# Attention and two expert layers in one kernel: the first block's q loaded in four DMAs instead of one, and k and v of batch 1 loaded on 128 partitions instead of 96

## The chip, the core and the metric

The kernel runs on one core of a Trainium2 chip, as one launch. The metric is the device time of that launch in microseconds (us). Engines are named as the profile names them: PE (matmuls), PEld (weight loads of PE), DVE, ACT, POOL, and SP, which here only issues DMAs.

## The reference

What is computed, cut to what matters (batch 4, 8 heads, 576 positions, head size 64; 2304 tokens, width 512, inner widths 2048 and 1024, all in float32):

```python
kv = einsum('bhsd,bhse->bhde', k, v)
out = einsum('bhsd,bhde->bhse', q, kv)
x = out / sqrt(mean(out * out, -1) + 1e-06) * g_norm    # then heads side by side: 2304 x 512
h = x @ w_in
x = (h * tanh(log1p(exp(h)))) @ w_out                   # 512 -> 2048 -> 512
h = x @ w2_in                                           # 512 -> 1024
solu = h * softmax(h)
return layernorm(solu) * g_ln @ w2_out                  # 1024 -> 512
```

## The kernel before

**Tiling.** The 2304 tokens are cut into six blocks of 384 (`BLK`), three tiles of 128 each. A batch has 576 positions, so block 0 lies in batch 0, and block 1 takes the end of batch 0 and the start of batch 1. Every large matmul is done as three float16 passes on a high and a low half of each operand (`PASS`).

**The start, block 0.** k and v of a batch come in four pairs of heads, (b, 0) to (b, 3), each two DMAs of 288 KB (`load_pair`, L238 to L249). For a batch in `WIDE` (L168, batch 0 alone) a head's 576 rows lie on 64 partitions, nine rows on each, so that two heads fill 128 partitions and a partition gets one run of 2304 bytes; `kv_pair` (L273 to L287, matmuls L286) then does 18 float32 matmuls of 64 rows by 64 columns. For the other batches the rows lie on 96 partitions, six on each, for both heads: two runs of 1536 bytes and 12 matmuls of 96 rows. Block 0's q is one DMA of 768 KB for all eight heads (`load_q`, L253). For each pair of heads c, PE transposes q (qTp, L317), multiplies it with kv (xoT, L331), sums the squares (L342), spreads the inverse root (rT<-ident,rho, L362, after POOL's power at L354, which follows DVE's small addition at L348), and DVE multiplies (xf, L373) and takes low halves (xT, L382).

**The start, block 1 on.** q of block 1 is two DMAs of 384 KB, which wait until all of block 0's q has been transposed. ACT makes its high halves (qhl, L398), DVE the low ones (L403), and SP issues a transposing DMA for each of the three tiles (L411). kv of batch 1 becomes two float16 halves (kvr, L297 and L303), PE multiplies (xo, L424), a norm follows on ACT, DVE and POOL (L435 to L465), and a second transposing DMA per tile (L475) brings it to the layout that the first expert layer reads.

**Weights.** w_in and w_out come in pieces of 512 KB (st, L489 and L497), which ACT (L534), POOL (L539) and DVE (L544, L551) decode, and ACT (L562) and DVE (L571 and L569) split into halves. The first w_in pieces serve eight groups of hidden columns of block 0: 12 matmuls each (hp, L593). Blocks 1 and 2 follow, with the second matmul (y, L633) in between, then the rest; the second expert layer is L710 and L793.

**What sets the order.** `Plan` holds every step as a task with an engine, a guessed cost, and what it waits for. `search` orders the tasks by due times, then tries 300 random shifts of the early ones and keeps an order whenever PE's planned end is no later. Each engine then runs its own list strictly in that order, so a waiting instruction holds all that stands behind it. `plan.line` (L1064) fixes the order of the first loads on SP. The plan's guessed times also set how many idle matmuls on the identity fill PE's gaps (`keep_warm`, L1057, called at L1092 and L1094). A change of a cost or of a dependence can so move any early instruction on any engine.

Of the kernel before, what the change touches and what calls it, by code (L numbers as in the profile page):

```python
# [8 lines left out]
FP32 = mybir.dt.float32  # L9
# [27 lines left out]
class Plan:  # L37
# [4 lines left out]
    def add(self, key, engine, cost, fn, after=(), lag=0.1, due=None):  # L42
        assert key not in self.tasks, key
        self.tasks[key] = [engine, cost, fn, [a for a in after if a is not None], lag, due]
# [96 lines left out]
def tile_attn_moe_moe2(  # L141
# [13 lines left out]
    nc = tc.nc  # L155
    B, H, S, D = q.shape
# [4 lines left out]
    R = 3  # L161
    BLK = 128 * R
# [2 lines left out]
    G = 4  # L165
    NT2 = NTOK // 128
    K2 = F2 // 128
    WIDE = (0,)  # L168
    K1, K2R = 2 * S // 128, S // 96
    PASS = ((0, 0), (0, 1), (1, 0))  # L170
    NST, NDEC, NG, NM = 5, 5, 3, 3
# [9 lines left out]
    gs = const.tile([128, 1], FP32, name="gs")  # L181
    gl = const.tile([128, K2], FP32, name="gl")
    nhalf = const.tile([128, H, 1], FP32, name="nhalf")
    ident = const.tile([128, 128], FP32, name="ident")
# [16 lines left out]
    at = at_cm.__enter__()  # L201
# [36 lines left out]
    def load_pair(b, i):  # L238
        t = yT[RAW[b][i]].rearrange("p c a t -> p (c a t)").bitcast(FP32)
        if b in WIDE:  # L240
            t = t[:, 0:2 * K1 * D].rearrange("p (a r d) -> p a r d", a=2, r=K1)
# [3 lines left out]
        for a, src in enumerate((k, v)):  # L245
            s = src[b, 2 * i:2 * i + 2]
            s = s.rearrange("h (p r) d -> (h p) r d", r=K1) if b in WIDE else s.rearrange(
                "h (p r) d -> p h r d", r=K2R)
            nc.sync.dma_start(out=t[:, a], in_=s)  # L249

    q_t = {}

    def load_q(b):  # L253
        t = at.tile([128, H, R, D], FP32, tag="qraw", name="qraw")
        t0 = b * BLK
        done = 0
        while done < BLK:
            bb, s = divmod(t0 + done, S)
            n = min(BLK - done, S - s)
            nc.sync.dma_start(  # L260
                out=t[done // R:(done + n) // R],
                in_=q[bb, :, s:s + n, :].rearrange("h (p r) d -> p h r d", r=R),
            )
            done += n
        q_t[b] = t
# [7 lines left out]
    def kv_pair(b, i):  # L273
# [7 lines left out]
        kvp_t[b] = p  # L281
        n = K1 if b in WIDE else K2R
        for r in range(n):
            for h in range(2):
                kh, vh = (t[HALF[h], a, r] if b in WIDE else t[:, a, h, r] for a in range(2))
                nc.tensor.matmul(  # L286
# [520 lines left out]
    def task(key, engine, cost, fn, args, after=(), lag=0.1, due=None):  # L807
        add(key, engine, cost, lambda: fn(*args), after, lag, due)

        for tag in taken:  # L810
            if tag in taker:
                plan.line([taker[tag], key])
            taker[tag] = key
        taken.clear()

    taken, taker = [], {}
    LAND, PAIR, QLD, PIECE = 2.0, 2.15, 3.0, 1.6
# [24 lines left out]
    def load_gl():  # L842
        nc.sync.dma_start(out=gl, in_=g_ln.rearrange("(k p) -> p k", p=128))

    task(("gs",), "A", 1.0, load_gs, (), [("ldq", 0)], 4.0)
    task(("gl",), "S", 1.5, load_gl, (), [("ld", ("2", 15))], 4.0)


# [2 lines left out]
    def ring(tag, bufs, user):  # L851

        users = rings.setdefault(tag, [])
        users.append(user)
        if bufs > 1:
            taken.append(tag)
        return [users[-1 - bufs]] if len(users) > bufs else []
# [11 lines left out]
    for b in range(B):  # L869
        for i in range(4):  # L870
            task(("kv", b, i), "P", 1.27 if b in WIDE else 0.92, kv_pair, (b, i),
                 [("ld", b, i), ("kv", b, i - 1) if i else None], 0.25)
# [3 lines left out]
    for i in range(4):  # L876
        plan.tasks["kv", 0, i][3] += ring("a", 1, ("kvf", 0, i))
        task(("kvf", 0, i), "A", 0.3, kv_full, (0, i), [("kv", 0, i), ("zero",)], 0.2)
    task(("ldq", 0), "S", QLD, load_q, (0,), (), LAND)
    for c in range(4):  # L880
        u = (0, c)
        bank = f"y{c % 3}"
        task(("qT", *u), "P", 0.95, e_qT, u,
             [("ldq", 0), ("ident",)] + ring(bank, 1, ("qc", *u)), 0.25)
        task(("qc", *u), "A", 0.49, e_qc, u, [("qT", *u)] + (
            ring("qT", 3, ("xo", *u)) if c < 3 else ring("xhl", 2, ("xo", *u))))
    for c in range(4):
        u = (0, c)
        bank = f"y{c % 3}"
# [31 lines left out]
    for b, r in tiles:  # L921
        u = (b, r)
# [21 lines left out]
    for b, grp in units:  # L944
        T0 = nominal["H", b, grp]
        for i in range(G):
            w = [("wlo", ("1", grp * G + i))]
            bank = ring("h", 3, ("mi", b, grp, i))
# [28 lines left out]
    for n, (b, grp) in enumerate(units):  # L977
# [3 lines left out]
        for j in range(4):  # L981
            w = [("wlo", ("2", grp * G + i)) for i in ((j,) if turn else range(G))]
            gg = [("glo", b, grp, j // 2)] if turn else [("glo", b, grp, i) for i in range(2)]
            bank = []
# [33 lines left out]
    for t in range(NT2):  # L1018
        y = [("ylo", t // R, c) for c in range(C)]
        w = [("wlo", ("3", j)) for j in range(8)]  # L1020
# [16 lines left out]
        w = [("wlo", ("4", j)) for j in range(8)]  # L1037
        bank = last_of[t] if t < 4 else [("oc", t - 4)]
# [18 lines left out]
    def keep_warm(n, p):  # L1057
# [4 lines left out]

    w, kv = (lambda f: ("ld", ("1", f))), (lambda b, i: ("ld", b, i))
    plan.line([  # L1064
        ("ldq", 0), kv(0, 0), kv(0, 1), w(0), kv(0, 2), kv(0, 3), w(1), w(2), w(3),
        ("ldq", 1), kv(1, 0), kv(1, 1), w(4), kv(1, 2), w(5), kv(1, 3), w(6), w(7),
    ])

    def setup(n):
# [59 lines left out]
```

## Time and profile before

| | |
|---|---|
| median of 3 runs | 632.7 us (632.59 to 633.2) |
| the profiled execution | 631.64 us |
| its span, first to last instruction | 629.8 us |
| PE busy | 616.5 us, 98% of the span |
| DVE, ACT, POOL busy | 311.2, 268.3, 97.3 us |
| DMA | 61.99 MB, mean 98 GB/s |

[...] Times count from the start of the span; 1.84 us of the execution lie outside it.

### The profile page before, as it was taken

The page shows a single profiled execution, that of the slowest core. Times are in us where ns is not written, and L with a number is a line of the kernel's source. Part 1 is how long each engine was busy: PE and PEld are TensorE (multiplying, and loading weights), DVE is VectorE, ACT ScalarE, POOL GpSimd, SP SyncE. Part 2 cuts the span into 40 slices and gives each one's busy share as a digit, 9 for nine tenths or more (in the row PEclk, how much of TensorE's full clock was granted, in tenths as well). Part 3 has the DMA queues.
Part 4 walks back from the last instruction along what each step waited for, and adds up shares of the span by engine and source line. Part 5 has one row for each costly group of instructions (what it writes and reads, how often), then busy time and mean ns, then how long its engine had stood idle before and what let it go on. Part 6 is the DMA issues. An engine that isn't in the chain of part 4 may idle for free.

```text
span 629.8 us, 9947 instructions
## 1 busy us (share of the span) xinstructions
PE 616.5 (98%) x4079; PEld 353.2 (56%) x4079; DVE 311.2 (49%) x534; ACT 268.3 (43%) x459; POOL 97.3 (15%) x126
## 2 busy tenths in 40 slices
PE   8798999999999999999999999999999999999997
PEld 6566566666666666666666666654444444444443
DVE  1578778783113351334213278937777245555410
ACT  4557766663322333333333266525444233333311
POOL 1426442320000210012101133200011000000000
PEclk9899999999999999999999999999999999999999
DMA  8998864825103360004100274201430533333331
GB/s 295 251 225 218 227 175 127 256 79 101 50 1 111 91 127 0 1 18 84 19 1 2 50 250 168 101 0 35 68 67 1 112 89 69 83 74 77 80 105 51
DMA packets 98429, 61.99 MB, mean 98 GB/s; under 512 B 72016, under 2 KB 90960, under 8 KB 98384
## 3 DMA queue, kind: packets, MB, share of 16 engines
q1 hardware_dynamic: 98224, 61.36, 38.8%
q8 instruction: 32, 0.52, 0.3%
q14 instruction: 13, 0.11, 0.1%
q10 hardware_dynamic: 160, 0.00, 0.0%
HBM read 39.33 MB, written 4.72 MB: 70 GB/s over the span
## 4 chain that ended last, share of the span: by engine, by line
PE 92%; DMA 5%; DVE 2%; SPq 1%; issue 0%; ACT 0%; ACTq 0%; DVEq 0%
PE y L633 30%; PE hp L593 28%; PE op L793 15%; PE h L710 15%; PE kvp L286 2%; DMA yT<-in_v_dram 2%; PE xo L424 1%; DMA st<-in_moe_w_out_dram 1%; DMA qraw<-in_q_dram 1%; DMA xT<-xhl 1%; SPq L260 0%; PE qTp L317 0%; DVE P L551 0%; DVE w L571 0%; DVE st L544 0%
## 5 line engine op out<-in xcount | busy, mean ns | idle before, releaser
L633 PE MATMUL y<-g,w 128*128 128x384 f16 x1152 | 201.0, 326 | 0.0
L593 PE MATMUL hp<-xT,w 128*128 128x384 f16 x960 | 167.9, 327 | 2.4 <-DMA xT<-xhl 1.5
L593 PEld LDWEIGHTS <-w 128*128 128x128 f16 x1152 | 111.9, 98 | 76.9 <-DVE w L571 1.9
L633 PEld LDWEIGHTS <-w 128*128 128x128 f16 x1152 | 111.7, 98 | 74.2
L603 ACT ACTIVATE m<-hp 128x384 f32<-128x384 f32 x96 | 46.7, 489 | 122.5 <-PE hp L593 121.1
L710 PE MATMUL h<-w,yT 128*128 128x512 f16 x432 | 96.0, 379 | 0.0
L793 PE MATMUL op<-w,lnT 128*128 128x512 f16 x432 | 95.2, 379 | 0.0
L615 DVE SCALAR_TENSOR_TENSOR g<-m,g 128x768 f16<-128x768 f32 x48 | 46.4, 970 | 92.7 <-ACT g L610 92.4
L793 PEld LDWEIGHTS <-lnT 128*128 128x128 f16 x432 | 42.3, 98 | 50.7
L710 PEld LDWEIGHTS <-yT 128*128 128x128 f16 x432 | 42.3, 98 | 50.1
L539 POOL TENSOR_SCALAR st<-st 128x512 f32<-128x512 f32 x48 | 45.6, 960 | 102.2 <-ACT P L534 98.3
L610 ACT ACTIVATE g<-m 128x768 f16<-128x768 f32 x48 | 40.0, 838 | 12.2 <-PE y L633 11.6
L534 ACT ACTIVATE P<-st 128x512 f32<-128x512 f32 x48 | 32.3, 676 | 23.7 <-DMA st<-in_moe_w_in_dram 14.2
L727 ACT ACTIVATE e<-h,nb 128x1024 f32<-128x1024 f32 x18 | 20.1, 1116 | 51.4 <-DVE nb L722 30.6
L544 DVE SCALAR_TENSOR_TENSOR st<-st 128x512 int32<-128x512 int32 x48 | 36.0, 769 | 10.7 <-POOL st L539 10.6
L444 POOL TENSOR_SCALAR ms<-ms 128x8 f32<-128x8 f32 x15 | 4.3, 289 | 208.5 <-DVE ms L439 208.2
L551 DVE SCALAR_TENSOR_TENSOR P<-P,st 128x512 int32<-128x512 int32 x48 | 35.6, 769 | 0.0
L593 PE MATMUL hp<-yT,w 128*128 128x384 f16 x192 | 32.5, 326 | 0.0
L721 DVE TENSOR_REDUCE mx<-h 128x1 f32<-128x1024 f32 x18 | 22.0, 1224 | 20.3 <-PE h L710 20.3
L760 POOL TENSOR_SCALAR var<-var 128x1 f32<-128x1 f32 x18 | 3.5, 192 | 178.8 <-DVE var L755 178.8
L734 DVE SCALAR_TENSOR_TENSOR z<-h,e 128x1024 f32<-128x1024 f32 x18 | 22.0, 1225 | 17.8 <-ACT e L727 17.8
L778 DVE TENSOR_TENSOR hl<-z,hl 128x1024 f16<-128x1024 f32 x18 | 22.0, 1224 | 14.8 <-ACT hl L774 14.8
(95 smaller groups left out, 438.3 us busy)
## 6 DMA issues: line engine op xcount, KB each, us to landing
st<-in_moe_w_in_dram SPq DMA_DIRECT2D x24, 512.0 KB, 5.6
st<-in_moe_w_out_dram SPq DMA_DIRECT2D x24, 512.0 KB, 4.6
yT<-in_k_dram SPq DMA_DIRECT2D x16, 288.0 KB, 5.9
yT<-in_v_dram SPq DMA_DIRECT2D x16, 288.0 KB, 6.5
out_dram<-osb SPq DMA_DIRECT2D x18, 256.0 KB, 2.8
qraw<-in_q_dram SPq DMA_DIRECT2D x4, 768.0 KB, 5.8
qraw<-in_q_dram SPq DMA_DIRECT2D x4, 384.0 KB, 9.5
lnT<-hl SPq DMA_TRANSPOSE x18, 4.3
```

The source lines that it names most:

```text
L534: nc.scalar.activation(out=P, in_=v[:, :, 1], func=ACTF.Copy, scale=2.0 ** -111)
L539: nc.gpsimd.tensor_scalar(out=v[:, :, 1], in0=v[:, :, 1], scalar1=0.0, scalar2=1.0, op0=ALU.mult, op1=ALU.mult)
L544: nc.vector.scalar_tensor_tensor(out=v[:, :, 0], in0=v[:, :, 0], scalar=29, in1=v[:, :, 1], op0=ALU.logical_shift_right, op1=ALU.bitwise_or)
L551: nc.vector.scalar_tensor_tensor(out=P.bitcast(I32), in0=P.bitcast(I32), scalar=3, in1=v[:, :, 0], op0=ALU.logical_shift_left, op1=ALU.bit ...
L593: nc.tensor.matmul(out=h_t[b, grp, i], lhsT=w1[:, c, wa, f:f + 128], rhs=xT_t[b][:, C * xa + c], start=(c == 0 and m == 0), stop=(c == C - ...
L603: nc.scalar.activation(out=m_t[b, grp, i // 2][:, i % 2], in_=h_t.pop((b, grp, i)), func=ACTF.Mish, scale=2.0 ** -16)
L610: nc.scalar.activation(out=g_t[b, grp][:, 0, 2 * i:2 * i + 2], in_=m_t[b, grp, i], func=ACTF.Copy, scale=64.0)
L615: nc.vector.scalar_tensor_tensor(out=g_t[b, grp][:, 1, j], in0=m_t.pop((b, grp, i)), scalar=64.0, in1=g_t[b, grp][:, 0, j], op0=ALU.mult, ...
L633: nc.tensor.matmul(out=y_t[cc][:, 0:BLK], lhsT=w2[:, grp * G + ii, wa, cc * 128:(cc + 1) * 128], rhs=g_t[b, grp][:, ga, ii], start=(first ...
L710: nc.tensor.matmul(out=hp[:, half], lhsT=y[:, c, ya, tok], rhs=w3[:, c, wa, half * 512:(half + 1) * 512], start=(m == 0), stop=(m == 3 * C ...
L721: nc.vector.reduce_max(out=mx, in_=T[t, "hp"], axis=AX.X)
L793: nc.tensor.matmul(out=op, lhsT=lnT[:, K2 * la + kk], rhs=w4[:, kk, wa], start=(m == 0), stop=(m == 3 * K2 - 1),)
```

## The change

`WIDE` becomes (0, 1), so batch 1 is loaded and multiplied as batch 0 was: DMAs of 128 partitions with runs of 2304 bytes, and 18 matmuls for a pair of heads where there were 12. Block 0's q is loaded by a new function in four DMAs of 192 KB, one per two heads, into the same tile, and each transposing step waits for its own quarter alone. On SP the first pair of k and v stands behind the first quarter, the second pair between the third quarter and the fourth. Everything else that differs comes from the plan, which is searched anew.

```diff
-    WIDE = (0,)
+    WIDE = (0, 1)
...
+    def load_q0(c):
+
+        if 0 not in q_t:
+            q_t[0] = at.tile([128, H, R, D], FP32, tag="qraw", name="qraw")
+        nc.sync.dma_start(
+            out=q_t[0][:, 2 * c:2 * c + 2],
+            in_=q[0, 2 * c:2 * c + 2, 0:BLK, :].rearrange("h (p r) d -> p h r d", r=R))
...
-    task(("gs",), "A", 1.0, load_gs, (), [("ldq", 0)], 4.0)
+    task(("gs",), "A", 1.0, load_gs, (), [("lq0", 0)], 4.0)
...
-    task(("ldq", 0), "S", QLD, load_q, (0,), (), LAND)
+    for c in range(4):
+        task(("lq0", c), "S", QLD / 4, load_q0, (c,), (), LAND)
...
-             [("ldq", 0), ("ident",)] + ring(bank, 1, ("qc", *u)), 0.25)
+             [("lq0", c), ("ident",)] + ring(bank, 1, ("qc", *u)), 0.25)
...
-        ("ldq", 0), kv(0, 0), kv(0, 1), w(0), kv(0, 2), kv(0, 3), w(1), w(2), w(3),
+        ("lq0", 0), kv(0, 0), ("lq0", 1), ("lq0", 2), kv(0, 1), ("lq0", 3), w(0),
+        kv(0, 2), kv(0, 3), w(1), w(2), w(3), ("ldq", 1), kv(1, 0), kv(1, 1), w(4),
```

Lines behind L252 stand 8 to 10 lower in the changed kernel.

On PE, at the first k and v pair of batch 1 (yT_102 is that pair's raw tile, yT_103 the second's; rT<-ident,rho spreads block 0's inverse roots, six matmuls for a pair of heads), before:

```order
L342 MATMUL rT<-ones,sq 128x2 x3
L362 MATMUL rT<-ident,rho 64x128 x6
L286 MATMUL kvp<-yT_102 64x64 x12
L593 LDWEIGHTS w_68
L593 MATMUL hp<-xT,w_68 128x384
...
L286 MATMUL kvp<-yT_103 64x64 x12
L362 MATMUL rT<-ident,rho 64x128 x6
```

and with the change:

```order
L601 LDWEIGHTS w_68
L601 MATMUL hp<-xT,w_68 128x384
...
L370 MATMUL rT<-ident,rho 64x128 x12
L294 MATMUL kvp<-yT_102 64x64 x18
L601 LDWEIGHTS w_68
L601 MATMUL hp<-xT,w_68 128x384
...
L294 MATMUL kvp<-yT_103 64x64 x18
```

The last spreading step of block 0, which stood behind both of batch 1's first pairs, now stands ahead of them.

On DVE at the same place (ms<-rT is the small addition ahead of POOL's power, kvr the low halves of kv of batch 0, qhl those of block 1's q, xf<-xf,rT the multiplication that needs rT), before:

```order
L348 TENSOR_SCALAR ms<-rT 128x6
L303 SCALAR_TENSOR_TENSOR kvr_91<-kvf,kvr_91 64x4x64 x2
L382 TENSOR_TENSOR xT<-xf,xT 128x384
L403 SCALAR_TENSOR_TENSOR qhl<-qraw,qhl 128x512 x2
L348 TENSOR_SCALAR ms<-rT 128x6
L382 TENSOR_TENSOR xT<-xf,xT 128x384
L551 SCALAR_TENSOR_TENSOR P<-P,st 128x512
L373 TENSOR_TENSOR xf<-xf,rT 128x384
```

and with the change:

```order
L356 TENSOR_SCALAR ms<-rT 128x6
L390 TENSOR_TENSOR xT<-xf,xT 128x384
L381 TENSOR_TENSOR xf<-xf,rT 128x384
L356 TENSOR_SCALAR ms<-rT 128x6
L311 SCALAR_TENSOR_TENSOR kvr_91<-kvf,kvr_91 64x4x64 x2
L411 SCALAR_TENSOR_TENSOR qhl<-qraw,qhl 128x512
L381 TENSOR_TENSOR xf<-xf,rT 128x384
L411 SCALAR_TENSOR_TENSOR qhl<-qraw,qhl 128x512
```

The fourth small addition stands ahead of the low halves of q instead of behind two of them.

On PE, where block 0's hidden groups end (hp on w_68; the y rows are the second matmul, xo on kvr_92 is block 2's product of q and kv), before:

```order
L1059 MATMUL hp<-ident 128x256
L593 LDWEIGHTS w_68
L593 MATMUL hp<-xT,w_68 128x384
...
L633 MATMUL y_958<-g,w_69 128x384
...
L424 MATMUL xo<-kvr_92,qT 128x128
```

and with the change:

```order
L432 MATMUL xo<-kvr_92,qT 128x128
...
L1068 MATMUL hp<-ident 128x256
L601 LDWEIGHTS w_68
L601 MATMUL hp<-xT,w_68 128x384
...
L641 MATMUL y_920<-g,w_69 128x384
```

Between the last idle matmuls and the first y there were 60 hp matmuls (block 0's last group and block 1's first four) and are now 24 (that group and block 1's first one); the first of block 2's xo products stands ahead of them instead of behind the first y. Behind this place the five idle matmuls that stood among the later y rows are gone, and no idle matmul comes after it.

## Rows read from the trace of the kernel before

**Rows 1.** The page: busy us of each engine, share, instructions.

```profile
PE 616.5 (98%) x4079; PEld 353.2 (56%) x4079; DVE 311.2 (49%) x534; ACT 268.3 (43%) x459; POOL 97.3 (15%) x126
```

**Rows 2.** Stages: length, busy of PE, PEld, DVE, ACT, POOL, PE's clock, DMA.

```profile
22.60:26.00 3.40, 1.70 (x18) 1.38 (x18) 0.56 (x1) 1.62 (x4) 1.94 (x2) 1.00 1.09 248
26.00:28.70 2.70, 0.00 (x1) 0.04 (x1) 1.74 (x4) 2.04 (x4) 0.23 (x1) 0.51 1.12 259
28.70:32.80 4.10, 4.10 (x41) 2.68 (x42) 2.42 (x5) 1.82 (x4) 1.27 (x1) 0.50 1.10 278
...
64.00:100.00 36.00, 36.00 (x249) 22.63 (x248) 27.49 (x39) 23.02 (x42) 15.42 (x16) 1.00 0.66 179
```

**Rows 3.** PE in order of time: start, length, line, operation, [idle before].

```profile
28.70 1.55 PE L286 MATMUL kvp<-yT 96*64 96x64 f32 x24 [2.73 <-DMA yT<-in_v_dram]
30.18 2.10 PE L593 MATMUL hp<-xT,w 128*128 128x384 f16 x6
32.21 1.20 PE L286 MATMUL kvp<-yT 96*64 96x64 f32 x24
33.24 0.82 PE L362 MATMUL rT<-ident,rho 128*64 128x128 f32 x12
34.44 1.14 PE L593 MATMUL hp<-xT,w 128*128 128x384 f16 x6
38.41 0.92 PE L286 MATMUL kvp<-yT 96*64 96x64 f32 x24
60.04 2.11 PE L593 MATMUL hp<-xT,w 128*128 128x384 f16 x12
63.63 7.97 PE L593 MATMUL hp<-xT,w 128*128 128x384 f16 x48 [1.47 <-DMA xT<-xhl]
```

**Rows 4.** DVE in order of time, the same columns.

```profile
26.96 1.29 DVE L403 SCALAR_TENSOR_TENSOR qhl<-qraw,qhl 128x512 f16<-128x512 f32 x2 [2.52 <-ACT qhl L398]
28.17 0.16 DVE L348 TENSOR_SCALAR ms<-rT 128x6 f32<-128x6 f32 x1
34.11 0.56 DVE L373 TENSOR_TENSOR xf<-xf,rT 128x384 f32<-128x384 f32 x1 [2.99 <-PE rT L362]
65.15 1.30 DVE L569 TENSOR_TENSOR w<-P,w 128x512 f16<-128x512 f32 x2 [1.38 <-ACT w L562]
```

**Rows 5.** POOL in order of time: the last two powers of block 0.

```profile
23.71 1.33 POOL L354 TENSOR_TENSOR rho<-ms,nhalf 128x6 f32<-128x6 f32 x1
28.47 1.50 POOL L354 TENSOR_TENSOR rho<-ms,nhalf 128x6 f32<-128x6 f32 x1 [3.43 <-DVE ms L348]
```

**Rows 6.** ACT in order of time: its two longest waits on loads.

```profile
22.36 0.66 ACT L534 ACTIVATE P<-st 128x512 f32<-128x512 f32 x1 [1.62 <-DMA st<-in_moe_w_in_dram]
26.30 1.67 ACT L398 ACTIVATE qhl<-qraw 128x512 f16<-128x512 f32 x3 [2.08 <-DMA qraw<-in_q_dram]
```

**Rows 7.** Stages as in rows 2; the last two columns are DMA share and GB/s.

```profile
9.90:13.10 3.20, 2.56 (x64) 2.00 (x58) 0.48 (x3) 1.16 (x4) 0.66 (x1) 1.00 1.07 411
...
22.70:25.20 2.50, 0.93 (x8) 0.85 (x10) 0.56 (x1) 1.52 (x4) 1.94 (x2) 1.00 1.09 242
```

**Rows 8.** SP's issue of block 1's last transposing DMA, and such DMAs' landing.

```profile
58.65 1.24 SPq L475 DMA_TRANSPOSE xT<-xhl  x1
...
DMA to landing us min/median/max: 3.1/3.4/5.0
```

**Rows 9.** PE later, in order of time; the last row is the chain's last piece.

```profile
73.39 0.83 PE L424 MATMUL xo<-kvr,qT 128*128 128x128 f16 x12
...
96.85 0.71 PE L1059 MATMUL hp<-ident 128*128 128x256 f16 x5
...
589.74 36.27 PE op L793 x168
```

**Rows 10.** PE early, in order of time.

```profile
1.35 4.93 PE L1059 MATMUL idle<-ident 128*128 128x256 f16 x25 [1.35 <-POOL ident L1072]
9.35 1.26 PE L286 MATMUL kvp<-yT 64*64 64x64 f32 x36
```

More of the change, by code (lines that the diff above doesn't have):

```diff
@@ L1064, in tile_attn_moe_moe2 @@
     plan.line([
-        ("ldq", 0), kv(0, 0), kv(0, 1), w(0), kv(0, 2), kv(0, 3), w(1), w(2), w(3),
-        ("ldq", 1), kv(1, 0), kv(1, 1), w(4), kv(1, 2), w(5), kv(1, 3), w(6), w(7),
+        ("lq0", 0), kv(0, 0), ("lq0", 1), ("lq0", 2), kv(0, 1), ("lq0", 3), w(0),
+        kv(0, 2), kv(0, 3), w(1), w(2), w(3), ("ldq", 1), kv(1, 0), kv(1, 1), w(4),
+        kv(1, 2), w(5), kv(1, 3), w(6), w(7),
     ])
```

## The prediction

> **What bounds the kernel now.** I read the page first. PE is busy for 616.5 of 629.8 us [rows 1], and its list is in strict order, so a microsecond is only to be had where PE stands still, runs idle matmuls or runs slowly. The stages say where: from 64 us PE is busy all the time (36.00 of 36.00) [rows 2], and the chain's last piece ends at 589.74 + 36.27 = 626.01 [rows 9]. Before that PE waits for other engines. So the end is the start of the 48 matmuls at 63.63 [rows 3] plus what PE still has to do from there, and the question is by how much that start moves and whether anything leaves or joins the rest.
>
> The reader should see four things ahead of 63.63. PE stands for 2.73 us until v of batch 1's first pair lands, at 28.70 [rows 3]. [...] DVE stands for 2.99 us until 34.11, because the last spreading step rT waits on PE behind two pairs of batch 1 and six hp matmuls; it starts at 33.24 [rows 3, 4]. And ACT is held by two loads, the fourth weight piece at 22.36 and q of block 1 at 26.30 [rows 6].
>
> **The change part by part.** *q in four.* The first transposing step can start when a quarter of q is there. I cost this at nothing: the same bytes stand ahead of the fourth weight piece and of block 1's q on DMA engines that are full (share 1.07 at 411 GB/s) [rows 7], so ACT's two waits end where they did, at 22.36 and 26.30 [rows 6], and all that block 0 gained is behind them. Three more issues on SP delay no transfer while the engines are full. If that cover failed by a gap in the transfers, each microsecond of gap would move both waits by one.
>
> *128 partitions for batch 1.* In the stretch with nothing but pairs of batch 0 (128 partitions) the engines move 411 GB/s, in the one with pairs of batch 1 (96 partitions) 242, with the share over 1 in both [rows 7]. A DMA of 288 KB (0.295 MB) then takes 0.72 instead of 1.22 us: 0.50 less each, 1.0 for the first pair, 4.0 for all eight. So PE's wait for the first pair ends at 27.7 instead of 28.70. [...]
>
> On PE a pair of batch 1 costs 1.26 instead of 0.92 us at the high clock [rows 10, 3], 4 x 0.34 = 1.36 more.
>
> *Moved work.* The fourth small addition of block 0 on DVE, at 28.17 behind the low halves of q [rows 4], now stands ahead of them. POOL's power for it, which ran at 28.47, can follow the third one, which ends at 23.71 + 1.33 = 25.04, and end at 26.5 [rows 5]. So rT, 0.82 long [rows 3], can be done on PE by 27.4, before the first pair lands at 27.7, and it now stands ahead of that pair. DVE's wait of 2.99 [rows 4] goes. What is late next is the work between that pair and the 48 matmuls, and I take it from two sides.
>
> - PE's side (the lesser gain). From 28.70 to the end of the fourth pair, 38.41 + 0.92 = 39.33, PE took 10.63 us [rows 3]. With the same low clock it now takes 10.63 - 0.82 (rT is out) + 1.36 = 11.17, and from 27.7 ends at 38.9: 0.4 earlier. Without the low clock the six hp matmuls take 1.14 instead of 2.10 and the two pairs 0.92 instead of 1.55 and 1.20 [rows 3]: 1.87 less, so 2.3 earlier.
> - DVE's side. It is freed of 2.99, but does one low half of block 2's q (1.29 / 2 = 0.65 [rows 4]) ahead of block 1's end: 2.3 earlier.
>
> Both feed the norm of block 1 and its last transposing DMA, issued at 58.65 [rows 8], for which the 48 matmuls wait [rows 3]. So their start gains between 0.4 and 2.3; no row lies nearer to either end, since half of it is the clock, and I take the middle, **1.4**. That DMA landed after 4.9 us, the median of its kind is 3.4 [rows 8]: at most 1.5 more, which I leave to the range, since PE is not through with the last hidden group of block 0, begun at 60.04 [rows 3], much before 62 anyway.
>
> *The rest of PE's work.* The 48 matmuls take 7.97 and twelve take 2.11 [rows 3], so one is 5.86 / 36 = 0.163 and 0.16 of a row is drain. The first xo product of block 2, 0.83 at 73.39, moves ahead of the start, into time in which PE ran idle matmuls; the five idle matmuls at 96.85, 0.71, are gone [rows 9]. Less the drain that is 0.67 + 0.55 = **1.2** off the rest.
>
> The sum is 1.4 + 1.2 = 2.6 us. The profiled execution took 631.64, so 629.0; the runs' median of 632.7 is 1.06 above it, and the prediction is against the median: 632.7 - 2.6 = **630.1**. By the bounds it is 0.4 + 1.2 = 1.6 (631.1) to 2.3 + 1.5 + 1.2 = 5.0 (627.7), the last only if all falls well at once.
>
> **The rivals.** *The clock falls in a worse place.* Before the first pair PE is again only partly busy, as it was in the 1.70 of 3.40 us before the fall [rows 2]. If a low stretch of the same 6.8 us (26.0 to 32.8) lies wholly over pairs and hp matmuls that others wait for, it costs half of it, 3.4, where 1.87 was paid: 1.5 more on the side of PE. Then 0.4 - 1.5 + 1.2 = 0.1: **632.6**, no change. For it speaks that the work is moved closer together behind a thin stretch; against it, that rT and three hp matmuls now fill a part of what was an empty 2.7 us [rows 2].
>
> *The 128-partition DMAs land no sooner.* Then PE still starts the first pair at 28.70, and 1.0 of the gain goes: 1.6, **631.1**. Against it stand the rates [rows 7]. [...]
>
> *A new wait behind the start.* The first y row now stands right behind 12 hp matmuls, at 62.2 + 1.95 = 64.2, instead of behind 48. It needs the first piece of w_out, whose low half DVE began at 65.15 and so ended at 65.8 [rows 4]. DVE does less ahead of it now, and earlier; if that brings nothing, PE waits 1.6 us: 1.0 left, **631.7**.
>
> *Slower: the clock stays low from the start.* The 25 idle matmuls at the start took 4.93 / 25 = 0.197 us each, the five late ones (0.71 - 0.16) / 5 = 0.11 [rows 10, 9]: PE begins at the low level and was brought up by a dense row. Only 7 idle matmuls stand there now, then a quarter's transposing, six more and gaps. If PE is not brought up before batch 1's first pair and stays low through the fourth, the 11.17 - 1.87 = 9.3 us of work there take 1.7 times that (a pair 1.55 to 0.92, hp 2.10 to 1.14 [rows 3]), 15.8, and end at 43.5 instead of 39.33: 4.2 late, less the 1.2. That is 3.0 slower, **635.7**. It decides at 27.7; a clock that is up by then costs nothing, since ACT's waits at 22.36 and 26.30 cover block 0. Against it: the pairs of batch 0 are dense work.
>
> **How the numbers follow.** Forecast 0.53, worse clock 0.15, DMAs no sooner 0.11, new wait 0.09, slower 0.10; 0.02 for more than the bounds give. What a measurement of this kernel can tell from no change is about 0.2%, 1.3 us: below 631.4 is faster, above 634.0 slower. The forecast and the DMA rival are faster (0.64), as are the 0.02 and a third of the new wait (0.03): 0.69. The worse clock and the rest of the new wait are the same: 0.21. Slower is 0.10. The range reaches from 628.0, little short of the far bound, to 632.7, which takes in all but the slower case.
>
> **What would show it.** Right: rT ahead of the first pair at about 27, PE's first pair at 27.7, GB/s near 400 while batch 1 loads, no DVE wait for rT, ACT's waits at 22.4 and 26.3 as before, the hp row of block 1 at about 62, and no PE wait behind it. The forecast is wrong if those two ACT waits move, if the granted clock is 0.5 in another stretch than 26 to 33, if a y row waits for DVE, or if xo of block 2, now ahead of the last hidden groups, waits for its transposing DMA.

## The result, and the profile after

The changed kernel takes 626.89 us (median of 4 runs, 626.78 to 627.83), the kernel before 632.64 (4 runs beside them, 632.16 to 633.2). The ratio is 0.9912, 95% interval 0.9895 to 0.9929: 5.75 us less, where 2.6 was forecast; the direction was right, the time lies 1.1 below the low end of the range. The profiled execution took 626.94 (span 624.8); before it was 631.64, so these two differ by 4.70.

PE of the changed kernel, in order of time (start, length, line, operation; equal ones that follow each other are merged, and brackets say how long the engine had been idle before a row and what ended that; lines are 8 to 9 higher than before):

```profile
24.42 1.23 PE L1068 MATMUL hp<-ident 128*128 128x256 f16 x5 [1.09 <-DVE xf L381]
25.44 1.16 PE L601 MATMUL hp<-xT,w 128*128 128x384 f16 x3
26.53 2.12 PE L370 MATMUL rT<-ident,rho 128*64 128x128 f32 x24
28.58 1.26 PE L294 MATMUL kvp<-yT 64*64 64x64 f32 x36
36.39 1.26 PE L294 MATMUL kvp<-yT 64*64 64x64 f32 x36
...
60.08 2.11 PE L601 MATMUL hp<-xT,w 128*128 128x384 f16 x12 [0.51 <-DMA xT<-xhl]
62.03 2.11 PE L641 MATMUL y<-g,w 128*128 128x384 f16 x12
...
69.83 0.83 PE L432 MATMUL xo<-kvr,qT 128*128 128x128 f16 x12
```

The stages of the changed kernel (length, busy of PE, PEld, DVE, ACT, POOL with counts, the clock that PE was granted as a share of the full one, DMA share, GB/s), and the last piece of the chain that ended last:

```profile
10.00:13.00 3.00, 3.00 (x64) 2.76 (x61) 0.13 (x1) 1.36 (x4) 0.00 (x0) 1.00 1.05 402
24.40:27.80 3.40, 3.38 (x20) 2.26 (x21) 1.48 (x4) 1.54 (x5) 1.98 (x2) 0.50 1.06 373
28.70:32.80 4.10, 4.10 (x83) 3.13 (x84) 4.10 (x8) 2.46 (x5) 0.91 (x1) 1.00 1.58 289
64.00:100.00 36.00, 36.00 (x239) 22.22 (x238) 28.17 (x42) 22.11 (x41) 14.91 (x14) 1.00 0.68 169
```

```profile
585.00 36.27 PE op L801 x168
```

ACT's two waits of [rows 6], now; then from DVE the fourth small addition, the multiplication that waited 2.99 for rT before, and the last low half of block 1's q:

```profile
22.08 0.68 ACT L542 ACTIVATE P<-st 128x512 f32<-128x512 f32 x1 [0.58 <-DMA st<-in_moe_w_in_dram]
26.28 1.15 ACT L406 ACTIVATE qhl<-qraw 128x512 f16<-128x512 f32 x2 [1.86 <-DMA qraw<-in_q_dram]
```

```profile
24.28 0.15 DVE L356 TENSOR_SCALAR ms<-rT 128x6 f32<-128x6 f32 x1
31.32 0.55 DVE L381 TENSOR_TENSOR xf<-xf,rT 128x384 f32<-128x384 f32 x1
32.94 0.69 DVE L411 SCALAR_TENSOR_TENSOR qhl<-qraw,qhl 128x512 f16<-128x512 f32 x1
```

Read against [rows 3, 9]: block 1's hp start at 60.08 for 63.63, which is 3.55 earlier. From there to the chain's last piece PE needs 585.00 - 60.08 = 524.92 for 589.74 - 63.63 = 526.11, which is 1.19 less. Together 4.74, the whole difference of the two profiled executions. The granted clock is 0.50 from 24.4 to 27.8, 3.4 us, in place of 0.51 and 0.50 for 6.8 us, from 26.0 to 32.8 [rows 2]. Until 26.38, when POOL's last power ends, rT could not start anyway; what the rest costs is tested below.

### The profile page after: what moved, and what is told of

The parts are those of the page before. It is cut to its first block, busy times and chain, and to the rows that moved or that the text cites. A ratio compares the mean times of both kernels' runs of the same rounds, so it can differ in the third digit from the quotient of the medians.

```text
span 624.8 us, 9988 instructions
## 1 busy us (share of the span) xinstructions
PE 616.5 (99%) x4103; PEld 353.7 (57%) x4103; DVE 310.9 (50%) x534; ACT 267.3 (43%) x459; POOL 95.5 (15%) x126
## 3 DMA queue, kind: packets, MB, share of 16 engines
HBM read 39.33 MB, written 4.72 MB: 70 GB/s over the span
## 4 chain that ended last, share of the span: by engine, by line
PE 92%; DMA 5%; ACT 2%; SPq 0%; DVE 0%; issue 0%; ACTq 0%
PE y L641 30%; PE hp L601 28%; PE op L801 15%; PE h L718 15%; DMA qraw<-in_q_dram 2%; DMA st<-in_moe_w_in_dram 2%; PE kvp L294 2%; PE xo L432 1%; DMA xT<-xhl 1%; DMA yT<-in_k_dram 1%; ACT P L542 0%; PE rT L370 0%; ACT qhl L406 0%; ACT xhl L468 0%; ACT g L618 0%; ACT m L611 0%
## 5 line engine op out<-in xcount | busy, mean ns | idle before, releaser
L547 POOL TENSOR_SCALAR st<-st 128x512 f32<-128x512 f32 x48 | 43.6, 918 | 101.5 <-ACT P L542 98.0
```

Source lines behind the costliest of these rows:

```text
L547: nc.gpsimd.tensor_scalar(out=v[:, :, 1], in0=v[:, :, 1], scalar1=0.0, scalar2=1.0, op0=ALU.mult, op1=ALU.mult)
```

## Where the 3.55 us come from: SP

The prediction looked at PE and DVE. The next two fences are SP, before and after, from the issue of the last load of batch 1 (v of the fourth pair) to the next weight piece: start, length of the issuing instruction, line, operation. In these rows SP issues nothing else while a transposing DMA's issue lasts.

```profile
28.58 0.31 SPq L249 DMA_DIRECT2D yT<-in_v_dram  x1
...
29.51 4.75 SPq L411 DMA_TRANSPOSE qT<-qhl  x1
...
34.37 3.20 SPq L411 DMA_TRANSPOSE qT<-qhl  x1
...
38.63 1.24 SPq L411 DMA_TRANSPOSE qT<-qhl  x1
...
39.96 1.19 SPq L489 DMA_DIRECT2D st<-in_moe_w_in_dram  x2
```

```profile
27.40 0.33 SPq L249 DMA_DIRECT2D yT<-in_v_dram  x1
...
28.16 2.71 SPq L419 DMA_TRANSPOSE qT<-qhl  x1
...
30.98 3.37 SPq L419 DMA_TRANSPOSE qT<-qhl  x1
...
34.53 1.88 SPq L419 DMA_TRANSPOSE qT<-qhl  x1
...
36.51 0.54 SPq L497 DMA_DIRECT2D st<-in_moe_w_in_dram  x1
...
55.19 1.23 SPq L483 DMA_TRANSPOSE xT<-xhl  x1
```

And from the view of that load's line, the time from the issue of that last v to its landing, before and after:

```profile
DMA to landing us min/median/max: 9.1/9.1/9.1
```

```profile
DMA to landing us min/median/max: 7.2/7.2/7.2
```

DVE's last low half of q in the kernel before, which the third transposing DMA needs:

```profile
37.33 1.14 DVE L403 SCALAR_TENSOR_TENSOR qhl<-qraw,qhl 128x512 f16<-128x512 f32 x1
```

The reader should see three things. The first two transposing issues of block 1's q last 4.75 and 3.20 us before, 2.71 and 3.37 after, where the third before is 1.24. The second ends, in both kernels, just ahead of the landing of the last load of batch 1: 37.57 against 28.58 + 9.1 = 37.7 before, 34.35 against 27.40 + 7.2 = 34.6 after. And the third could not follow at once before, because DVE finished the last low half of q only at 37.33 + 1.14 = 38.47; after, it was done at 32.94 + 0.69 = 33.63. So SP is through with the three at 36.41 instead of 39.87. The next weight piece moves by 3.45 (39.96 to 36.51), block 1's last transposing DMA by 3.46 (58.65 [rows 8] to 55.19), the hp by 3.55.

The wait for that last load ends in a thin tail in both kernels: from 35.5 to 37.0 before 27 GB/s at a DMA share of 0.16, from 33.0 to 34.0 after 25 GB/s at 0.06 (one of the 16 engines over which the profile counts the share would be 1 / 16 = 0.06). What leaves the tail no run shows.

SP is not the only path in the kernel before. The chain that the profile follows back from the end does not pass these three issues there. It goes from v of the first pair over PE's pairs, the fourth of which ends at 39.33, to DVE's steps up to 45.23, behind which SP issues a piece of w_out at 45.29; that piece lands at 51.84. ACT shows how close the two paths lie. It waits 1.06 for the first piece that SP issued behind the three, and later 0.35 for this piece of w_out:

```profile
44.23 0.68 ACT L534 ACTIVATE P<-st 128x512 f32<-128x512 f32 x1 [1.06 <-DMA st<-in_moe_w_in_dram]
...
51.95 0.67 ACT L534 ACTIVATE P<-st 128x512 f32<-128x512 f32 x1 [0.35 <-DMA st<-in_moe_w_out_dram]
```

In the changed kernel the chain does pass the third issue and the two loads behind it, then q of block 2, issued at 37.64:

```profile
46.22 1.15 ACT L406 ACTIVATE qhl<-qraw 128x512 f16<-128x512 f32 x2 [1.28 <-DMA qraw<-in_q_dram]
```

So for the kernel before it is not shown that SP alone set the time. This was a reading of two traces. The experiments test it.

## The experiments

All ratios are to the kernel before on the same chip. There its median was 631.1 to 631.6, with single runs from 629.3 to 633.6, so differences below about 0.7 us are not told apart.

### The order without the loads, the loads without the order, and another order

The changed kernel's order on 96 partitions (the planner keeps its price of a pair, the loads and matmuls change):

```diff
-    WIDE = (0, 1)
+    WIDE, PLANNED = (0,), (0, 1)
...
-            task(("kv", b, i), "P", 1.27 if b in WIDE else 0.92, kv_pair, (b, i),
+            task(("kv", b, i), "P", 1.27 if b in PLANNED else 0.92, kv_pair, (b, i),
```

> The changed kernel's order of work on every engine and its q in four, but k and v of batch 1 on 96 partitions again. If the gain is the order (block 1's tail on DVE and PE, what PE does while it waits), most of it stays: about 627.5, at most 628.5, with the first pair of batch 1 at about 28.7 and the first hp row of block 1 at 60.5 to 61. If it is the faster loading of batch 1, as the prediction had it, most of it goes: 630.5 or more, and that row at 62.5 or later.

The kernel before with the reverse, `WIDE, PLANNED = (0, 1), (0,)`:

> The order of the kernel before on every engine and q in one DMA, but k and v of batch 1 on 128 partitions. If the gain is the order, little of it appears: 631.5 to 632.6, with the first pair at about 27.7 (from 28.70) and block 1's hp row at 63 or so. If it is the faster loading, 628.5 to 630.

The first of these with q of block 0 in one DMA as well:

```diff
-        if 0 not in q_t:
-            q_t[0] = at.tile([128, H, R, D], FP32, tag="qraw", name="qraw")
+        if c:
+            return
+        q_t[0] = at.tile([128, H, R, D], FP32, tag="qraw", name="qraw")
         nc.sync.dma_start(
-            out=q_t[0][:, 2 * c:2 * c + 2],
-            in_=q[0, 2 * c:2 * c + 2, 0:BLK, :].rearrange("h (p r) d -> p h r d", r=R))
+            out=q_t[0],
+            in_=q[0, :, 0:BLK, :].rearrange("h (p r) d -> p h r d", r=R))
```

> The changed kernel's order of work on every engine with all loads as before: q of block 0 in one DMA, k and v of batch 1 on 96 partitions. If the order alone makes the gain, 627 to 628.5. If q in four pieces matters by itself, it is over 1 us slower than the kernel that differs from it only there. If the loads make the gain, about 632.6.

And the kernel before with `random.Random(3)` in the planner's search:

> The kernel before with nothing changed but the number that starts the planner's random search (3 for 1), so another order of the same work. If the gain is the order that the search happens to find, and could be had without the change, this one comes out at 627.5 to 630 (its planned end is 627.17, where the kernel before has 628.83 and the changed one 626.78). If the change itself makes it, it stays within 1.3 us of 632.6.

Measured: new order on 96 partitions 0.9970 (0.9958 to 0.9983), with q in one DMA too 0.9970 (0.9959 to 0.9980), old order on 128 partitions 0.9981 (0.9970 to 0.9991), another seed 0.9973 (0.9961 to 0.9984). So neither the order nor the loads make the gain alone: 1.9 and 1.2 us of it. Both theories as I had put them fall. The other seed, without the change, gets 1.7 us, 1.2 of it behind the start: in its trace PE needs 586.97 - 62.09 = 524.88 us from the start of block 1's hp to the last piece of the chain, as little as the changed kernel. That part of the gain is an order that the search may or may not find.

### The changed kernel again, and single causes

Run together: the changed kernel; the same with ten idle matmuls ahead of the first hp row; the kernel before with idle matmuls in its two waits; and the kernel before with only rT, its power and its small addition moved ahead.

> The changed kernel once more, beside other runs of the kernel before: what its gain is on this chip, as the measure for the three kernels run with it. The first measurement had 0.9912 of before; if single executions of either kernel scatter by a microsecond or two through the clock, the gain here is 3 to 6 us.

```diff
+        if key == ("H0", 0, 0):
+            keep_warm(10, warm)
         if engine == "P":
```

> The changed kernel with ten more idle matmuls (about 1.1 us of PE) in PE's wait before the first hp row of block 0, and nothing else. If the low clock that is left at 24.4 to 27.8 still costs time (rT at 2.12 for 24 matmuls where 12 take 0.88, the first pair begun 1.1 after it landed), the first pair starts near 27.5 and the kernel is 0.5 to 1 us faster than the changed kernel beside it. If that stretch lies where PE waits anyway, no difference (within 0.4).

```diff
+        if key in (("ms", 0, 3), ("kv", 1, 0)):
+            keep_warm(14 if key[0] == "ms" else 24, warm)
         if engine == "P":
```

> The kernel before with idle matmuls in PE's two long waits before batch 1 (14 ahead of 24.27, 24 ahead of 28.70), and nothing else. If the low clock over the pairs and hp rows of 28.70 to 32.8 is what the kernel before pays, by the prediction's 1.87 us, this one has no granted clock of 0.5 between 20 and 40, and is 1.5 to 2.5 us faster than before. If DVE's wait and the landing of the loads set the time instead, less than 0.7.

```diff
+    for key, other in (("eps", ("qlo", 1, 0)), ("pow", ("kv", 1, 0)), ("rT", ("kv", 1, 0))):
+        keys = [k for _, k in order]
+        at_, n = order.pop(keys.index((key, 0, 3))), keys.index(other)
+        order.insert(n, (order[n][0] - 0.88, (key, 0, 3)))
...
     for at_time, key in order:
```

> The kernel before with one thing moved: the fourth small addition of block 0 on DVE ahead of the low halves of q, its power on POOL behind it, and the fourth spreading step rT on PE ahead of batch 1's first pair instead of behind the second. All loads and all the rest as before. DVE's wait of 2.99 goes. If that wait was on the path, as in the prediction's side of DVE, it is 1 to 2.5 us faster than before; if PE's pairs set the time, 0.8 (rT's own length) or less.

Measured: the changed kernel 0.9906 (0.9893 to 0.9918), 625.49 us; with more idle matmuls 0.9909 (0.9896 to 0.9922); the kernel before with idle matmuls 0.9996 (0.9986 to 1.0007); with rT ahead 0.9992 (0.9981 to 1.0002). The gain repeats. The low clock that is left in the changed kernel costs nothing that shows. Keeping the clock up in the kernel before (a mean of 0.999 or 1.0 in each of its twelve executions, where the profiled one before had 0.995) is worth at most 0.9 us, not the 1.87 that the prediction put on it. And taking away DVE's wait of 2.99 alone is worth at most 1.2, by the medians nothing. Its trace suggests why. SP's three transposing issues, and DVE's last low half of q:

```profile
29.39 4.67 SPq L411 DMA_TRANSPOSE qT<-qhl  x1
...
34.16 3.21 SPq L411 DMA_TRANSPOSE qT<-qhl  x1
...
37.55 2.10 SPq L411 DMA_TRANSPOSE qT<-qhl  x1
```

```profile
35.97 0.68 DVE L403 SCALAR_TENSOR_TENSOR qhl<-qraw,qhl 128x512 f16<-128x512 f32 x1
```

The low half is done at 36.65, 1.8 earlier than before, but SP is in the second issue until 37.37 and through with the third at 39.65, where it was 39.87. By this reading the loads hold SP, and what DVE gained stands behind SP. Why the third issue then lasts 2.10, where it took 1.24 before, the trace does not say.

### Loads together with one thing more, and weight loads past the hold

The kernel before on 128 partitions with idle matmuls, and on 128 partitions with rT ahead (edits as above, but 12 idle matmuls in the second wait in place of 24):

> The order of the kernel before, k and v of batch 1 on 128 partitions, and idle matmuls in PE's two waits before batch 1 (14 and 12), so that the clock stays up. Theory: the 128-partition loads act through SP, whose first transposing DMA of block 1's q takes 2.7 to 2.9 us to issue instead of 4.7 to 5.3, so that all later loads are issued some 3 us earlier (sixth weight piece of w_in at about 36.9 instead of 39.96); without a low clock to give it back this is 2 to 3 us faster than before. Rival: the loads are worth no more than the 1.2 us of the same kernel without idle matmuls, and the low clock costs nothing, as in the kernel before with idle matmuls; then 0.8 to 1.6.

> The order of the kernel before with rT, its power and its small addition moved ahead (as in the run where that alone brought nothing), and k and v of batch 1 on 128 partitions. If SP is what holds the rest, the move now pays: the third transposing DMA no longer waits for DVE (it ends at about 36 instead of 36.8 with 128 partitions alone), and the kernel is 2 to 3.5 us faster than before. If the move is worth nothing by itself with either loading, 1 to 1.6.

Two weight loads moved on SP, in the kernel before and, with the first piece of w_out as the second, in the changed one:

```diff
+    for key, other in ((("ld", ("1", 6)), ("qT", 1, 0)), (("ld", ("1", 7)), ("qT", 1, 2))):
+        keys = [k for _, k in order]
+        order.insert(keys.index(other), order.pop(keys.index(key)))
     for at_time, key in order:
```

> The kernel before with two weight loads moved on SP and nothing else: the seventh piece of w_in ahead of the three transposing DMAs of block 1's q, the eighth ahead of the third of them. If the loads queued behind those three set block 1's norm (ACT waits for them at 44.23 and 46.39, then at 50.55 and 51.95, in the middle of block 1's high halves), it is 0.7 to 2 us faster than before, and these waits go. If the transposing DMAs are then held up by the weight loads by as much, and the products behind them set the time, within 0.5 or slower.

> The changed kernel with two weight loads moved on SP in the same way: the seventh piece of w_in ahead of the three transposing DMAs of block 1's q, the first piece of w_out ahead of the third of them. In the changed kernel ACT waits for q of block 2 at 46.22, which is issued behind these loads. If the landing of what SP issues behind the transposing DMAs is still what ends last, 0.5 to 1.5 us faster than the changed kernel (0.988 to 0.990 of before); if PE's pairs and the products set it now, no faster or slower by what the transposing DMAs lose.

Measured: 128 partitions with idle matmuls 0.9968 (0.9957 to 0.9979); with rT ahead 0.9953 (0.9941 to 0.9965); weight loads first in the kernel before 0.9991 (0.9977 to 1.0005), in the changed one 0.9937 (0.9916 to 0.9958; its median is 626.04). So 128 partitions and rT ahead, worth 1.2 and about 0 apart, are worth 3.0 together. In that trace SP's three issues are

```profile
27.00 2.94 SPq L411 DMA_TRANSPOSE qT<-qhl  x1
...
30.05 3.14 SPq L411 DMA_TRANSPOSE qT<-qhl  x1
...
34.46 1.23 SPq L411 DMA_TRANSPOSE qT<-qhl  x1
```

and SP is through at 35.69. Part of the 3.0 may be the clock: five of its six executions had a granted clock of 0.999 or 1.0, where with 128 partitions alone nine of twelve had 0.997 or less, and of those twelve the three at 0.999 or 1.0 took 628.5 to 629.0, the two lowest in clock 631.2 and 632.0. With idle matmuls, at 0.999 or 1.0 in all twelve, the 128 partitions are worth 2.0. How the 3.0 divide between SP and the clock stays open. Moving the weight loads brought nothing that can be told from no change in either kernel: it isn't these pieces alone that pass the delay on.

### The last loads alone

Here PE's wait for the first pair and SP's hold say different things. The changed kernel with the last two pairs of batch 1, or the last alone (`i == 3`), on 96 partitions:

```diff
+        wide = b in WIDE and not (b == 1 and i >= 2)
-        if b in WIDE:
+        if wide:
...
+        wide = b in WIDE and not (b == 1 and i >= 2)
-        n = K1 if b in WIDE else K2R
+        n = K1 if wide else K2R
```

> The changed kernel with the last two pairs of batch 1 (four of its eight loads) on 96 partitions again, the first two on 128; order of work as in the changed kernel. PE begins these pairs at 33.1 and 36.4, after they can have landed in either form, and each takes 0.34 less. If the gain of the loads is PE's wait for the first pair, as the prediction had it, nothing is lost (the ratio to before stays at 0.990 to 0.991). If it is SP, whose transposing DMAs are held until the last of these loads has landed, the second of them ends some 2 us later, the loads behind it are issued 2 us later, and the kernel is 1 to 2 us slower than the changed kernel (0.992 to 0.994).

> The same with the last pair of batch 1 alone on 96 partitions (two of the eight loads). By SP half as much: the second transposing DMA ends about 1 us later than in the changed kernel, and the kernel is 0.5 to 1 us slower than it (0.9915 to 0.9925 of before). By PE's wait for the first pair nothing is lost.

Beside them the changed kernel with q in one DMA, which serves as their measure, and with a longer search (`plan.search(4000, 8.0)`):

> The changed kernel with its order of work and batch 1 on 128 partitions, but q of block 0 in one DMA ahead of the first k and v pair. The prediction costed q in four at nothing, since ACT's waits for the fourth weight piece and for q of block 1 end where they did: then the ratio is that of the changed kernel, 0.990 to 0.991. If the earlier start of block 0 carries through to rT and with it to the first pair, 0.5 to 1.5 us slower than the changed kernel (0.992 to 0.993).

> The changed kernel with nothing changed but the number of turns of the planner's search (4000 for 300), so another order of the same work, with a planned end of 625.83 where the changed kernel has 626.78. If the planner's end tells the time, 1 us faster than the changed kernel (0.989 of before). If it does not, because its prices hold a load to be as long on 96 as on 128 partitions and a transposing DMA to be 1.3, within 1 us of it on either side.

Measured: q in one DMA 0.9911 (0.9895 to 0.9927), 625.55 us, the gain of the changed kernel; the last pair on 96 partitions 0.9945 (0.9931 to 0.9959), 627.94; the last two 0.9962 (0.9947 to 0.9976), 629.27. So loads that the first pair has nothing to do with cost 2.4 and 3.7 us, more than I expected for SP, and nothing was expected by PE's wait for the first pair. The longer search is at 0.9914 (0.9897 to 0.9931): the planner's end, 0.95 earlier, does not tell the time.

SP with q in one DMA, then with two pairs on 96 partitions:

```profile
26.97 2.89 SPq L420 DMA_TRANSPOSE qT<-qhl  x1
...
29.97 3.13 SPq L420 DMA_TRANSPOSE qT<-qhl  x1
...
33.28 1.88 SPq L420 DMA_TRANSPOSE qT<-qhl  x1
```

```profile
26.90 5.49 SPq L421 DMA_TRANSPOSE qT<-qhl  x1
...
32.51 3.72 SPq L421 DMA_TRANSPOSE qT<-qhl  x1
...
36.41 2.01 SPq L421 DMA_TRANSPOSE qT<-qhl  x1
```

And of the latter PE's last two pairs, the first load issued behind the three on ACT, and PE around the start of block 1's hp (22 matmuls, of which the last 12 are that row's, so it starts at 59.99 + 10 x 0.1625 = 61.62; twelve take 2.11, and less the prediction's drain of 0.16 that is 0.1625 for one):

```profile
32.93 0.92 PE L296 MATMUL kvp<-yT 96*64 96x64 f32 x24 [0.58 <-DMA yT<-in_v_dram]
...
36.58 0.92 PE L296 MATMUL kvp<-yT 96*64 96x64 f32 x24 [0.67 <-DMA yT<-in_v_dram]
...
59.99 3.75 PE L603 MATMUL hp<-xT,w 128*128 128x384 f16 x22 [0.29 <-DVE w L581]
```

```profile
43.38 0.67 ACT L544 ACTIVATE P<-st 128x512 f32<-128x512 f32 x1 [2.14 <-DMA st<-in_moe_w_in_dram]
```

With q in one DMA PE's fourth pair is

```profile
36.03 1.26 PE L295 MATMUL kvp<-yT 64*64 64x64 f32 x36
```

With two pairs on 96 partitions PE did wait for these pairs, 1.25 in all, but the narrower pairs take 0.34 less each, and the fourth ends at 37.50, where with q in one DMA it is 37.29: 0.2 later. SP is through 3.26 later (38.42 against 35.16), block 1's hp start 3.24 later (61.62 against 58.38), and the execution is 3.05 longer (628.41 against 625.36). So PE's pairs don't carry the difference. ACT may have waited among the slower loads as well, which no row here shows; but ahead of 43.38 it stands idle for 2.14 until the first piece issued behind the three lands (the row above), so a load that SP issued late ends last there. This is the clearest case for SP: the two traces start the first transposing issue at 26.90 and 26.97 and part behind it.

### All traces in one table

The start of block 1's hp against the end of the third transposing issue on SP, one profiled execution each (where the hp row runs on from the row ahead, its start is counted in matmuls of 0.1625):

| kernel | SP through | hp of block 1 | difference | execution |
|---|---|---|---|---|
| before | 39.87 | 63.63 | 23.8 | 631.64 |
| before, rT ahead | 39.65 | 63.81 | 24.2 | 631.90 |
| before, idle matmuls | 37.95 | 61.20 | 23.3 | 629.75 |
| old order, 128 | 36.81 | 58.99 | 22.2 | 628.47 |
| old order, 128, idle matmuls | 37.03 | 60.02 | 23.0 | 628.62 |
| old order, 128, rT ahead | 35.69 | 58.78 | 23.1 | 627.34 |
| new order, 96 | 38.96 | 61.77 | 22.8 | 628.54 |
| new order, 96, q whole | 38.87 | 61.73 | 22.9 | 628.71 |
| before, other seed | 39.66 | 62.09 | 22.4 | 629.12 |
| changed | 36.41 | 60.08 | 23.7 | 626.94 |
| changed, again | 34.30 | 58.10 | 23.8 | 624.88 |
| changed, idle matmuls | 35.96 | 58.98 | 23.0 | 625.78 |
| changed, longer search | 38.20 | 61.17 | 23.0 | 628.11 |
| changed, last two pairs 96 | 38.42 | 61.62 | 23.2 | 628.41 |
| changed, last pair 96 | 36.29 | 60.09 | 23.8 | 627.03 |
| changed, q whole | 35.16 | 58.38 | 23.2 | 625.36 |
| before, weight loads moved | 42.41 | 62.85 | 20.4 | 630.91 |
| changed, weight loads moved | 36.59 | 59.30 | 22.7 | 626.13 |

But for the kernel before with its weight loads moved, SP's end spans 5.6 us, the difference 22.2 to 24.2, over several orders of PE and DVE. (In the execution of the old order on 128 partitions the rest behind block 1's hp took 0.9 us more than in the two others of that order on 128, for which its trace names no cause.)

Two things limit what the table shows. Each row is one execution, not the kernel's time: those of the old order on 128 partitions and of the kernel before with idle matmuls are the fastest of their twelve (medians 629.84 and 630.78), that of the longer search is the slowest of its six (median 626.67). And a start that is earlier as a whole moves both columns: between the two executions of the changed kernel the first transposing issue is 2.0 apart (28.16 and 26.15), SP's end 2.1 and the time 2.06. So the table shows that the two columns move together; that the loads make the difference is shown by the runs with pairs on 96 partitions.

With the weight loads moved in the kernel before, SP is through 2.5 later than before, but two pieces already stand ahead of the third issue, and block 1's hp start 0.8 earlier. So the end of the third issue does not set the start by itself; the loads that stand behind it count too. Which of the things that SP issues behind the three, or the three products of their data, carries the delay differs by kernel (ACT waits 2.14 for a weight piece with two pairs on 96 partitions and not there with q in one DMA). That is left open.

## Why the prediction was right and wrong

**Right.** The bound: PE's strict list, so that the end is the start of block 1's hp plus the rest. **The rest**: 1.2 forecast, 1.19 found, by the steps named (xo of block 2 ahead of the start, no five idle matmuls at 96.85). **q in four at nothing**: ACT's waits end at 22.08 and 26.28 [rows 6], and with q in one DMA the gain is the same. **No new wait**: y follows hp at 62.03 with no gap, and PE is busy for 36.00 of 36.00 from 64 on. **The landing** of the first pair: v landed at 17.04 + 10.4 = 27.4, 1.1 earlier, where 1.0 was forecast. rT stands ahead of the first pair, DVE's wait of 2.99 is gone (the third multiplication waits 0.41 for its rT), and the rate while batch 1 loads is 373 GB/s from 24.4 to 27.8 where it was 259 from 26.0 to 28.7 [rows 2]; from 28.7 to 32.8, where the transposing DMAs begin, it is 289 for 278. These runs don't tell how much of that is the number of partitions: with it the run on each changed too, from 1536 to 2304 bytes.

**Wrong in a detail.** The low clock moved: it lies at 24.4 to 27.8, and the prediction had named a granted clock of 0.5 outside 26 to 33 as a sign against it. It is shorter, and ten more idle matmuls ahead of it bring nothing, so it did not become the price of the rival. The first pair began at 28.58, not 27.7: rT's two last groups stand ahead of it, 24 matmuls in 2.12 at the low clock, from 26.53, when POOL's powers were done. The ground of the slower rival was there at the start: behind seven idle matmuls the first pair of batch 0 took 2.19 us at 6.95, where it took 1.26 before, and a granted clock of 1.00 stands beside both. But at 11.31 the second took 1.26, so PE was up long before batch 1; what makes the early rows slow, the granted clock does not show. PE's fourth pair ended at 37.65, 1.7 earlier, within the bounds of PE's side; that is less than half of the 3.55.

**The step that failed** is in the part on 128 partitions. It worked out that the eight DMAs save 4.0 us and then used 1.0 of it, the first pair's, because PE was seen to wait for that pair. The other six were taken as free, since PE begins their pairs later. The queue that the loads share with what follows was not looked at, though the term ended in a DMA that SP issues. The last load lands 3.1 us earlier (34.6 for 37.7), the second transposing issue ends 3.2 earlier, the third 3.46, and block 1's last transposing DMA is issued 3.46 earlier. The term of the sum for the start, 1.4, with a far bound of 2.3, measured 3.55. The 1.5 us of a shorter landing, which I had allowed for beyond, did not come (4.8 from issue to landing, 4.9 before).

The split was wrong too. The 1.87 us for the clock and DVE's 2.99 were each taken for a price that the kernel pays; undone alone in the kernel before, each gives nothing that can be told. DVE's part may be real once the loads are short: on 128 partitions the third transposing issue starts at 34.46 with rT ahead and at 35.58 without, one trace each.

**The rest of the miss** is 1.0 us of measurement. I set the sum made in a profiled execution against the median of the runs and kept the distance between them, 1.06, for the changed kernel. Its profiled execution lies 0.05 above its median instead. The 631.64 of the kernel before lies below all four of its runs (632.16 to 633.2), so most of the 1.06 looks like chance in one execution. The four runs of each kernel lie 1.04 and 1.05 apart, so they do not show that one scatters more than the other.

## What to carry to other kernels

When loads get faster, don't price only the consumer that is seen to wait for the first one: follow the queue that issues them to the next instruction there whose issue lasts until they are nearly through (here the second transposing DMA, 0.1 to 0.3 us ahead of the last landing), and to what is queued behind it. An engine's wait that is removed alone and brings nothing may still be part of a gain; ask which other engine is late at the same place, and undo both together. And a sum made in one execution is a forecast for such an execution: a distance to the median that one execution happened to have should not be carried over to another kernel.

## What was not expected of the hardware

The shortest issues of a transposing DMA on SP took 1.23 or 1.24 us, where the loads were over. The first of three behind loads of batch 1 took 2.70 to 2.94 where all eight were on 128 partitions, 3.30 where the last two of them were on 96, and 4.67 to 5.49 where the last four or all eight were. With a weight piece put ahead as well the first two together took 6.96 for 6.20 in the changed kernel and 8.58 for 8.06 in the kernel before. In eight traces where nothing was put between these loads and the transposing DMAs (before, before with rT ahead, old order on 128 with rT ahead, changed, changed again, q whole, the last pair and the last two pairs on 96), the second one's issue ended 0.1 to 0.3 us ahead of the last load's landing. The longer search put its first transposing DMA on SP at 33.96, when that load was 1.7 to 1.9 us from landing, and there it took 1.35:

```profile
33.96 1.35 SPq L419 DMA_TRANSPOSE qT<-qhl  x1
```

SP is through no earlier for that (38.20), and its ratio, 0.9914, is that of the changed kernel. No version here beat the changed kernel by more than the runs can tell.
